# Loading the channel weights beside attention in three parts, in a fused attention, token-mixing and gating kernel

## The chip, the cores and the metric

One core of a Trainium2 chip runs the whole program. The metric is the device time in microseconds of one execution, as the median of several runs.

## What is computed

The input is attention over 2 batches of 12 heads (448 tokens, head size 64), then two mixing blocks. Cut to what matters here:

```python
x = attention(q, k, v)                                   # (2, 448, 768), causal
h = np.maximum(x.transpose(0, 2, 1) @ w_tok1, 0.0) @ w_tok2
u = x + h.transpose(0, 2, 1)
h2 = np.maximum(u @ w_ch1, 0.0) @ w_ch2                  # w_ch1: 768 x 1536
x = u + h2
# then a gated block with w_in, w_sg, w_out, and a residual
```

The first factor, `r = relu(u @ w_ch1)`, is what the change touches.

## The kernel before

Weights arrive as 64-bit words. `load_raw` (L104) issues one load of such words from SyncE's queue into a tile `wraw`, of which there are two. `decode` (L117) makes 32-bit numbers of them in a tile `wm` (three of them): an activation on ScalarE (L127), a shift on VectorE (L130) and a shift with an or on VectorE (L131). `load64` (L133) then makes a high part on ScalarE (L140) and, through `sub` (L100), a low part on GpSimd (L101). `load_w` (L143) does so for a slice of 128 columns of `w_ch1`: 128 partitions of 768 words, which is 768 KB of raw words, and gives `whi` and `wlo`.

`channel_up` and `up_third` multiply such a slice with `u`, which is kept as a high and a low part too, in `mm3` (L181): for each of six blocks `c` of 128 rows three matmuls, high by high (L185), high weight by low `u` (L186) and low weight by high `u` (L187), 18 in all into the PSUM tile `r_ps`.

Attention goes by pairs of heads. A head has two calls of `probabilities` (L324): scores on TensorE into `s_ps` (L345, two buffers), a mask with a running minimum on VectorE (L350), an exponential on ScalarE (L359), a half-precision high part on ScalarE (L371), its low part on GpSimd (L372, tile `hl`), and a transpose by DMA from SyncE's queue (L373) into `pT`. `values` (L383) multiplies `pT` with the values into `x_ps` (L396 to L398). At the end of a pair VectorE scales `x_ps` into `xf` (L424 to L426), and ScalarE and GpSimd split it into `xh` and `xl` (L429, L435, L101). After two pairs `token_mix` (L438) multiplies these into `a_ps` (L443, L444, and L185 to L187 from `mm3`), splits the result into `ah` and `al` (L448, L449) and multiplies again into `u_ps` (L459 to L468).

Eight of the twelve slices of `r` for batch 0 (`NF0`) are put beside the attention of batch 1. `up_third` (L495) is called from the fourth head of batch 1 on and multiplies two of the six blocks at a time. A scheduler orders the instructions of each engine by priorities and a timeline of its own. `tc.issue_after(ins)` adds an edge without a semaphore: what the block traces on the engine of `ins` stands behind `ins` on that engine. `marks` holds, for each head, the last DMA transpose issued by then; the load of slice `m` stands behind `marks[H - 2 + m]`. `tc.high_priority(offset=-LATER)` gives the load, the decode and the split of the slice a late priority.

Of the kernel before, what the change touches and what calls it, by code (L numbers as in the profile page):

```python
# [11 lines left out]
F32 = mybir.dt.float32  # L12
# [16 lines left out]
def mixer_kernel(  # L29
# [18 lines left out]
    nc = tc.nc  # L48
    B, H2, D2, S = q.shape
    H, D = 2 * H2, D2 // 2  # L50
# [3 lines left out]
    P = 128  # L54
# [5 lines left out]
    WC = 768  # L60
# [3 lines left out]
    LATER = 1500  # L64
# [5 lines left out]
    wpool = ctx.enter_context(tc.tile_pool(name="wpool", bufs=2))  # L70
# [29 lines left out]
    def sub(lo, src, hi):  # L100
        nc.gpsimd.tensor_sub(lo, src, f32(hi))  # L101
# [38 lines left out]
            nc.scalar.copy(hi, m)  # L140
        sub(lo, m, hi)

    def load_w(src, pool=wpool, bufs=3):  # L143

        k = src.shape[1]
        hi = pool.tile([P, WC // P, P], F32R, tag="whi", name="whi", bufs=bufs)[:, :k, :]
        lo = pool.tile([P, WC // P, P], F32R, tag="wlo", name="wlo", bufs=bufs)[:, :k, :]
        load64(hi.rearrange("p a f -> p (a f)"), lo.rearrange("p a f -> p (a f)"), src.rearrange("p a f -> p (a f)"))
        return hi, lo

    def absmax(dst, src):
# [65 lines left out]

    r_of = {}

    def channel_up(m, batches, pool, psum):  # L220

        wh, wl = load_w(w_ch1[m])
        for b in batches:
            us = slice(b * S, (b + 1) * S)
            pr = psum.tile([P, 512], F32, tag="d", name="r_ps")
            mm3(pr[:, :S], [((wh[:, c, :], wl[:, c, :]), (u_hi[c][b], u_lo[c][b])) for c in range(NCC)])
            r_done(m, b, pr, pool)
# [23 lines left out]
    with ExitStack() as at:  # L251
# [75 lines left out]
        def probabilities(qp, k2, hd, half, on_pe):  # L327

            ps = ps_s.tile([P, NP], F32, tag="s", name="s_ps")
            if (hd, half) == (1, 0):
                pe, mx = pes[count[0] % len(pes)], mxs[count[0] % len(pes)]
            else:
                pe = xp.tile([P, NP], F32, tag="pe", name="pe", bufs=NPE)
                mx = stp.tile([P, 2], F32, tag="mx", name="mx")
            todo, o = [], 0
            for j, i in enumerate(HALVES[half]):
                w = KW[i]
                if i > 0 or hd == 0:  # L340
                    todo.append((j, i, slice(o, o + w)))
                    q0 = S - 64 if i == 0 else S + w - P if hd else w - P - 64
                    for ks in KEYS[i]:
                        m = ks.stop - ks.start
                        last_s[0] = nc.tensor.matmul(ps[:, o:o + m], qp[:, q0:q0 + P], k2[:, ks], start=True, stop=True).ins  # L345
                        o += m
                else:
                    o += w
            for j, i, cs in todo:
                last_mx[0] = nc.vector.tensor_tensor_reduce(  # L350
                    out=pe[:, cs], in0=ps[:, cs], in1=mask0 if i == 0 else mask[:, MASKS[i]],
                    scale=-1.0 / math.sqrt(D), scalar=3.0e38, op0=ALU.add, op1=ALU.min, accum_out=mx[:, j:j + 1],
                ).ins
            bias = mx
            if not on_pe:
                bias = stp.tile([P, 2], F32, tag="bias", name="bias")
                nc.scalar.add(bias, mx, math.log(PSCALE))
            for j, i, cs in todo:
                nc.scalar.activation(pe[:, cs], pe[:, cs], AF.Exp, bias=bias[:, j:j + 1], scale=-1.0)  # L359
            pT = hlp.tile([P, 2, NP // P, P], F16, tag="pT", name="pT", bufs=4)  # L360
            if on_pe:
                tp = ps_e.tile([P, 512], F32, tag="d", name="t_ps")
                for c in range(NP // P):
                    cs = slice(c * P, (c + 1) * P)
                    nc.tensor.matmul(tp[:, cs], pe[:, cs], ident, is_transpose=True, start=True, stop=True)
                hi, lo = (pT[:, i].rearrange("p c q -> p (c q)") for i in range(2))
                nc.scalar.activation(hi, tp, AF.Copy, scale=PSCALE)
                nc.vector.scalar_tensor_tensor(lo, tp, PSCALE, hi, ALU.mult, ALU.subtract)
                return pT
            hl = hlp.tile([P, 2, NP], F16, tag="hl", name="hl", bufs=4)  # L370
            nc.scalar.copy(hl[:, 0], pe)  # L371
            nc.gpsimd.tensor_sub(hl[:, 1], pe, hl[:, 0])  # L372
            last[0] = nc.sync.dma_start_transpose(  # L373
                out=pT.rearrange("p a c q -> p (a c) q"), in_=hl.rearrange("p a n -> p (a n)")
            ).ins
            return pT


# [92 lines left out]
                nc.vector.tensor_sub(u_lo[cc][b], pu[:, :S], f32(u_hi[cc][b]))  # L471


        last, last_x, marks = [None], [None], []
        order = [(b, h) for b in range(B) for h in range(H)]
        qks, vss = {}, {}

# [14 lines left out]
        dense = list(range(NF0))  # L492
        thirds = []

        def up_third():  # L495

            if not thirds:
                m = dense.pop(0)
                with tc.issue_after(marks[H - 2 + m]), tc.high_priority(offset=-LATER):
                    wh, wl = load_w(w_ch1[m])  # L500
                pr = ps_e.tile([P, 512], F32, tag="d", name="r_ps")
                thirds.extend((m, pr, wh, wl, c) for c in range(0, NCC, 2))
            m, pr, wh, wl, c0 = thirds.pop(0)
            mm3(
                pr[:, :S],
                [((wh[:, c, :], wl[:, c, :]), (u_hi[c][0], u_lo[c][0])) for c in (c0, c0 + 1)],
                c0 > 0, not thirds,
            )
            if not thirds:
                r_done(m, 0, pr, rpool)  # L510

        def up():

            m = dense.pop(0)
            with tc.issue_after(marks[H - 2 + m]):
                channel_up(m, [0], rpool, ps_e)

        def decode_tok(c):
            with tc.issue_after(last_mx[0]), tc.high_priority(offset=-80):
# [11 lines left out]
        for n, (b, h) in enumerate(order):  # L531
            if n > 0:
                prepare(n + AHEAD)
                prepare_v(n + VAHEAD)
            if n == GH - 1:
                for c in range(2, NQ):
                    load_tok(c)
                for c in range(NT):
                    load_tok2(c)
            if h % GH == 0:  # L540
                x = (
                    xp.tile([P, GH // 2, 7, D], F32, tag="xf", name="xf", bufs=2),
                    xp.tile([P, NQ, GH * D], F32R, tag="xh", name="xh"),
                    xp.tile([P, NQ - 1, GH * D], F32R, tag="xl", name="xl"),
                )
            if h % 2 == 0:
                it = pair(b, h // 2, h % GH // 2, qks[b, h // 2], x, b == 0 and h > 0)
            next(it, None)
            marks.append(last[0])
            if h % GH == GH - 1:  # L550
                token_mix(b, h // GH, *x)

            if b == 1 and h >= 3:
                for _ in range(1 if h < H - 3 else 2):
                    up_third()
# [354 lines left out]
```

## Time and profile before

| | |
|---|---|
| runs before | 416.0, 416.13 and 414.38 us, median 416.0 |
| profiled execution | 416.44 us, its span 414.7 us |
| TensorE busy | 391.3 us (94%), mean granted clock 0.988 |
| GpSimd busy | 202.5 us (49%) |
| VectorE and ScalarE busy | 282.4 us (68%) and 250.4 us (60%) |

The profile is one execution. Its span leaves out 1.74 us of the time around it. The attention of both batches takes the first 169 us or so; after it come the other slices of `r`, the second channel product and the gated block. Shares over the whole span mix these stages, so they are read by stretches of time.

### The profile page before, as it was taken

Reading aid. Unit: us, or ns where it says so; the run is one execution under the profiler, and the core shown is the slowest. Engines: PE = TensorE matmul, PEld = TensorE weight load, DVE = VectorE, ACT = ScalarE, POOL = GpSimd, SP = SyncE. Lnnn points to the kernel's source line nnn. Section 1 sums busy time; section 2 is a strip of 40 time slices with the busy share of each in tenths; the row PEclk is TensorE's granted clock in tenths of the full one; section 3 lists DMA queues with packets and bytes.
Section 4 is the critical chain, followed back from the end, with each engine's and each line's share of the span. In section 5 each row is a group of like instructions: output and inputs, shape, how many; then the busy total and the mean of one; then the engine's idle time right before and its main releaser. Section 6 shows DMA issues by size and latency. Waiting matters only on the chain.

```text
span 414.7 us, 7332 instructions
## 1 busy us (share of the span) xinstructions
PE 391.3 (94%) x2622; PEld 267.9 (65%) x2622; DVE 282.4 (68%) x696; ACT 250.4 (60%) x483; POOL 202.5 (49%) x208
## 2 busy tenths in 40 slices
PE   5879899799898998999999999999999999999996
PEld 3447778588787887999889555555544445554554
DVE  6887866887785426444446787557898996469742
ACT  3988767787876555565679886344256556553210
POOL 3759864997686466062261447145121348315300
PEclk9999999799999999999999999999999999999999
DMA  7999899979997544466643313534623131100122
GB/s 220 246 238 232 161 206 271 246 186 236 265 247 140 137 112 144 163 217 229 207 149 102 90 65 114 186 107 134 222 73 90 51 103 51 52 2 0 68 92 107
DMA packets 61747, 61.77 MB, mean 149 GB/s; under 512 B 47888, under 2 KB 53264, under 8 KB 61712
## 3 DMA queue, kind: packets, MB, share of 16 engines
q1 hardware_dynamic: 61712, 61.32, 55.6%
q8 instruction: 20, 0.33, 0.3%
q14 instruction: 15, 0.12, 0.1%
HBM read 47.29 MB, written 2.75 MB: 121 GB/s over the span
## 4 chain that ended last, share of the span: by engine, by line
PE 25%; DVE 18%; ACT 12%; POOL 10%; DMA 9%; issue 8%; SPq 0%; POOLq 0%; ACTq 0%
DMA wraw<-in 7%; PE r_ps L186 5%; PE r_ps L185 5%; PE r_ps L187 5%; ACT r L172 3%; POOL hl L372 3%; PE o_ps L187 2%; PE o_ps L185 2%; PE o_ps L186 2%; DVE y L173 2%; DVE wm L131 2%; DVE w2m L131 1%; ACT wm L127 1%; PE u_ps L459 1%; POOL w L179 1%
## 5 line engine op out<-in xcount | busy, mean ns | idle before, releaser
L345 PE MATMUL s_ps<-k,q 128*128 128x64 f32 (+3 forms) x216 | 57.2, 405 | 11.5 <-DVE mx L350 4.8
L372 POOL TENSOR_TENSOR hl<-pe,hl 128x512 f16<-128x512 f32 x43 | 52.3, 1223 | 25.6 <-ACT hl L371 24.5
L101 POOL TENSOR_TENSOR wlo<-wm,whi 128x768 fp32r<-128x768 f32 x20 | 39.9, 1994 | 40.4 <-ACT whi L140 40.2
L185 PE MATMUL r_ps<-uh,whi 128*128 128x448 f32 x144 | 55.1, 383 | 0.0
L130 DVE TENSOR_SCALAR wm<-wm 128x768 int32<-128x768 int32 (+2 forms) x35 | 22.9, 655 | 46.9 <-ACT wm L127 46.9
L186 PE MATMUL r_ps<-ul,whi 128*128 128x448 f32 x144 | 53.9, 374 | 0.0
L187 PE MATMUL r_ps<-uh,wlo 128*128 128x448 f32 x144 | 53.0, 368 | 0.0
L185 PE MATMUL y_ps<-r,w 128*128 128x448 f16 x144 | 50.8, 353 | 0.0
L127 ACT ACTIVATE wm<-wraw 128x768 f32<-128x768 f32 (+2 forms) x35 | 27.8, 798 | 38.0 <-DMA wraw<-in 24.1
L186 PE MATMUL y_ps<-r,w 128*128 128x448 f16 x144 | 50.7, 352 | 0.0
L187 PE MATMUL y_ps<-r,w 128*128 128x448 f16 x144 | 50.6, 352 | 0.0
L345 PEld LDWEIGHTS s_ps<-k,q 128*128 128x128 f32 x216 | 32.2, 207 | 22.5 <-DVE mx L350 6.7
L350 DVE CUSTOM_DVE_ANT_0 pe<-s_ps,mask 128x192 f32<-128x192 f32 (+3 forms) x84 | 34.6, 441 | 7.2 <-PE s_ps L345 6.4
L246 POOL TENSOR_TENSOR y<-yt,ul 128x448 f32<-128x448 f32 x12 | 15.8, 1319 | 46.4 <-DVE yt L244 46.4
L359 ACT ACTIVATE pe<-pe,bias 128x448 f32<-128x448 f32 (+3 forms) x74 | 35.6, 525 | 0.4
L131 DVE SCALAR_TENSOR_TENSOR wm<-wraw,wm 128x768 int32<-128x768 int32 (+2 forms) x35 | 32.8, 938 | 0.7
L396 PE MATMUL x_ps<-vh,pT 128*128 128x65 f16 (+1 forms) x240 | 26.9, 201 | 3.1 <-DMA pT<-hl 3.0
L371 ACT CAST hl<-pe 128x512 f16<-128x512 f32 x43 | 26.3, 611 | 5.9 <-DMA pT<-hl 4.7
L185 PEld LDWEIGHTS r_ps<-uh,whi 128*128 128x128 f32 x144 | 27.3, 190 | 3.0 <-issue 0.4
L186 PEld LDWEIGHTS r_ps<-ul,whi 128*128 128x128 f32 x144 | 27.2, 189 | 3.1 <-issue 0.6
L187 PEld LDWEIGHTS r_ps<-uh,wlo 128*128 128x128 f32 x144 | 27.2, 189 | 2.7 <-issue 0.2
L179 POOL TENSOR_TENSOR w<-w2m,w 128x768 f16<-128x768 f32 x12 | 21.2, 1787 | 15.8 <-ACT w L178 11.2
(212 smaller groups left out, 1016.0 us busy)
## 6 DMA issues: line engine op xcount, KB each, us to landing
wraw<-in SPq DMA_DIRECT2D x36, 768.0 KB, 4.5
wraw<-in SPq DMA_DIRECT2D x14, 512.0 KB, 3.8
vr<-in SPq DMA_DIRECT2D x12, 320.0 KB, 4.0
k<-in SPq DMA_DIRECT2D x12, 224.0 KB, 3.7
q<-in SPq DMA_DIRECT2D x24, 112.0 KB, 4.0
out<-ob SPq DMA_DIRECT2D x11, 224.0 KB, 1.9
wraw<-in SPq DMA_DIRECT2D x3, 256.0 KB, 4.6
pT<-hl SPq DMA_TRANSPOSE x43, 4.0
```

What stands on the lines that cost most here:

```text
L101: nc.gpsimd.tensor_sub(lo, src, f32(hi))
L127: nc.scalar.activation(m, words.bitcast(F32)[:, :, 1], AF.Prelu, scale=2.0 ** -112, alpha=-(2.0 ** 32))
L131: nc.vector.scalar_tensor_tensor(mi, words[:, :, 0], 29, mi, ALU.logical_shift_right, ALU.bitwise_or)
L185: nc.tensor.matmul(ps, lh, rh, start=i == 0 and not begun, stop=False)
L186: nc.tensor.matmul(ps, lh, rl, start=False, stop=False)
L187: done.append(nc.tensor.matmul(ps, ll, rh, start=False, stop=ended and i == n - 1).ins)
L345: last_s[0] = nc.tensor.matmul(ps[:, o:o + m], qp[:, q0:q0 + P], k2[:, ks], start=True, stop=True).ins
L350: last_mx[0] = nc.vector.tensor_tensor_reduce(out=pe[:, cs], in0=ps[:, cs], in1=mask0 if i == 0 else mask[:, MASKS[i]], scale=-1.0 / math. ...
L359: nc.scalar.activation(pe[:, cs], pe[:, cs], AF.Exp, bias=bias[:, j:j + 1], scale=-1.0)
L371: nc.scalar.copy(hl[:, 0], pe)
L372: nc.gpsimd.tensor_sub(hl[:, 1], pe, hl[:, 0])
L396: nc.tensor.matmul(o, ph, vh[:, c, h, :D + 1], start=j == 0, stop=False)
```

## The change

`load_parts` is new. With `behind` given, `load_w` loads a slice in three parts of 256 words per partition, each behind a DMA transpose of its own, and these three transposes follow each other. The raw tile is the same, and so are `decode` and the high part: one operation each over 768 columns. The low part is made by three operations of 256 columns. `marks` now holds the place in the list `turns` of all transposes, and `turns_from(n)` gives three of them from there on. This holds for the eight slices beside attention; all other weights are loaded as before.

```diff
+    def load_parts(src, behind):
+        raw = wpool.tile([P, WC], mybir.dt.int64, tag="wraw", name="wraw", bufs=2)
+        w = WC // len(behind)
+        for i, ins in enumerate(behind):
+            cs = slice(i * w, (i + 1) * w)
+            with tc.issue_after(ins):
+                nc.sync.dma_start(raw[:, cs], src[:, cs])
+        return raw
...
-    def load_w(src, pool=wpool, bufs=3):
+    def load_w(src, pool=wpool, bufs=3, behind=None):
...
-        load64(hi.rearrange("p a f -> p (a f)"), lo.rearrange("p a f -> p (a f)"), src.rearrange("p a f -> p (a f)"))
+        src, hi1, lo1 = (t.rearrange("p a f -> p (a f)") for t in (src, hi, lo))
+        if behind is None:
+            load64(hi1, lo1, src)
+        else:
+            m = wpool.tile([P, WC], F32, tag="wm", name="wm", bufs=3)
+            decode(m, src, raw=load_parts(src, behind))
+            nc.scalar.copy(hi1, m)
+            w = WC // len(behind)
+            for i in range(len(behind)):
+                cs = slice(i * w, (i + 1) * w)
+                sub(lo1[:, cs], m[:, cs], hi1[:, cs])
...
-            last[0] = nc.sync.dma_start_transpose(
+            turns.append(nc.sync.dma_start_transpose(
...
+        def turns_from(n):
+            return [turns[min(marks[n] + i, len(turns) - 1)] for i in range(3)]
+
         def up_third():
...
-                with tc.issue_after(marks[H - 2 + m]), tc.high_priority(offset=-LATER):
-                    wh, wl = load_w(w_ch1[m])
+                with tc.high_priority(offset=-LATER):
+                    wh, wl = load_w(w_ch1[m], behind=turns_from(H - 2 + m))
...
-            with tc.issue_after(marks[H - 2 + m]):
-                channel_up(m, [0], rpool, ps_e)
+            channel_up(m, [0], rpool, ps_e, turns_from(H - 2 + m))
...
-            marks.append(last[0])
+            marks.append(len(turns) - 1)
```

Since the scheduler sets the order, the diff shows little of what moves. Three places follow. The numbers behind the names tell buffers apart; lines past L143 are those of each kernel's own file (L373 before is L393 now, L113 for these loads is L150).

**Place 1**, SyncE's queue and then VectorE, where the first slices are loaded, at about 63 to 79 us of the profile. `wraw_1667` holds slice 0, `wraw_1932` (now `wraw_1936`) slice 1, `wraw_2228` slice 2. The queue before:

```order
L113 DMA wraw_1667<-in_5 128x768
L113 DMA wraw_1932<-in_5 128x768
L306 DMA vr_1467<-in_2 128x640
L298 DMA k2_1463<-in_1 128x448
L373 DMA_TRANSPOSE pT_1343<-hl_1344 128x8x128
L373 DMA_TRANSPOSE pT_1378<-hl_1379 128x8x128
L300 DMA q0_163<-in_0 64x448
L113 DMA wraw_2228<-in_5 128x768
L373 DMA_TRANSPOSE pT_1404<-hl_1405 128x8x128
L373 DMA_TRANSPOSE pT_1433<-hl_1434 128x8x128
```

and now:

```order
L150 DMA wraw_1667<-in_5 128x256 x2
L150 DMA wraw_1936<-in_5 128x256
L326 DMA vr_1467<-in_2 128x640
L318 DMA k2_1463<-in_1 128x448
L393 DMA_TRANSPOSE pT_1343<-hl_1344 128x8x128
L393 DMA_TRANSPOSE pT_1378<-hl_1379 128x8x128
L320 DMA q0_163<-in_0 64x448
L150 DMA wraw_1667<-in_5 128x256
L150 DMA wraw_1936<-in_5 128x256
L393 DMA_TRANSPOSE pT_1404<-hl_1405 128x8x128
L393 DMA_TRANSPOSE pT_1433<-hl_1434 128x8x128
```

Three parts stand ahead of the first two transposes instead of two whole loads, and two parts ahead of the next two instead of a whole load. VectorE before (`wm_1666` and `wm_1931` are the decodes of slices 0 and 1, `s_ps_1480` and `s_ps_1514` are scores):

```order
L130 TENSOR_SCALAR wm_1666<-wm_1666 128x768
L131 SCALAR_TENSOR_TENSOR wm_1666<-wraw_1667,wm_1666 128x768
L471 TENSOR_TENSOR ul2_0_110<-u_ps_932,uh2_0_98 128x448
L313 TENSOR_REDUCE am_1469<-vr_1467 128x1
L130 TENSOR_SCALAR wm_1931<-wm_1931 128x768
L424 TENSOR_SCALAR rd_1249<-x_ps_1126,sv_968 128x7
L318 TENSOR_REDUCE sv_1322<-vm_1320 128x1
L131 SCALAR_TENSOR_TENSOR wm_1931<-wraw_1932,wm_1931 128x768
L350 ISA pe_1481,mx_1482<-s_ps_1480,mask0_86 128x64
```

and now:

```order
L446 TENSOR_TENSOR xf_974<-x_ps_1126,rd_1249 128x448
L370 ISA pe_1481,mx_1482<-s_ps_1480,mask0_86 128x64
L370 ISA mx_1482 128x1
L340 RECIPROCAL sv_1322<-sv_1322 128x1
L370 ISA pe_1481,mx_1482<-s_ps_1480,mask_87 128x448
L370 ISA mx_1482 128x1
L130 TENSOR_SCALAR wm_1666<-wm_1666 128x768
L370 ISA pe_1515,mx_1516<-s_ps_1514,mask_87 128x192
```

The decodes of slices 0 and 1 stood ahead of the masks of `s_ps_1480`; now slice 0 stands behind these masks, ahead of those of `s_ps_1514`, and slice 1 comes later still.

**Place 2**, GpSimd, where the low parts of slices 2 and 3 meet the attention of the third pair of batch 1 (its `x_ps` is number 1700 before, 1704 now), at about 85 to 104 us of the profile. Before, with `wlo_2226` for slice 2:

```order
L101 TENSOR_TENSOR wlo_2226<-wm_2227,whi_2225 128x768
L372 TENSOR_TENSOR hl_1527<-pe_1515,hl_1527 128x512
L372 TENSOR_TENSOR hl_1553<-pe1_156,hl_1553 128x512
L372 TENSOR_TENSOR hl_1582<-pe_1570,hl_1582 128x512
L372 TENSOR_TENSOR hl_1713<-pe_1702,hl_1713 128x512
L372 TENSOR_TENSOR hl_1748<-pe_1736,hl_1748 128x512
L372 TENSOR_TENSOR hl_1780<-pe0_155,hl_1780 128x512
L372 TENSOR_TENSOR hl_1809<-pe_1797,hl_1809 128x512
```

and now, with `wlo_2234` for slice 2 and `wlo_2336` for slice 3:

```order
L101 TENSOR_TENSOR wlo_2234<-wm_2235,whi_2233 128x256 x3
L101 TENSOR_TENSOR xh_1329<-xf_1328,xh_1329 64x64
L392 TENSOR_TENSOR hl_1717<-pe_1706,hl_1717 128x512
L101 TENSOR_TENSOR xl_1330<-xf_1328,xh_1329 128x3x128
L392 TENSOR_TENSOR hl_1752<-pe_1740,hl_1752 128x512
L101 TENSOR_TENSOR wlo_2336<-wm_2337,whi_2335 128x256 x3
L392 TENSOR_TENSOR hl_1784<-pe0_155,hl_1784 128x512
L455 TENSOR_SCALAR xh_1329<-xf_1328 64x64 x2
L392 TENSOR_TENSOR hl_1813<-pe_1801,hl_1813 128x512
```

The four low parts of the third pair stood in a row; now the low parts of two slices, and splits of `xf`, stand among them. The three operations of a slice follow each other here, as they do for all eight slices.

**Place 3**, GpSimd and then TensorE at the last token mix (`xh_2083`, now `xh_2091`), at about 156 to 166 us of the profile. GpSimd before (`wlo_2566` is slice 7; the next two are slices 0 and 1 for batch 1):

```order
L372 TENSOR_TENSOR hl_2376<-pe_2364,hl_2376 128x512
L101 TENSOR_TENSOR wlo_2566<-wm_2567,whi_2565 128x768
L101 TENSOR_TENSOR wlo_2661<-wm_2662,whi_2660 128x768
L435 TENSOR_SCALAR xh_2083<-xf_2082 64x64 x2
L101 TENSOR_TENSOR xh_2083<-xf_2082,xh_2083 64x64
L101 TENSOR_TENSOR wlo_2692<-wm_2693,whi_2691 128x768
```

and now (`wlo_2559` is slice 6, `wlo_2594` slice 7):

```order
L101 TENSOR_TENSOR wlo_2559<-wm_2560,whi_2558 128x256 x3
L455 TENSOR_SCALAR xh_2091<-xf_2090 64x64 x2
L101 TENSOR_TENSOR xh_2091<-xf_2090,xh_2091 64x64 x2
L101 TENSOR_TENSOR xl_2092<-xf_2090,xh_2091 128x3x128
L101 TENSOR_TENSOR wlo_2594<-wm_2595,whi_2593 128x256 x3
L101 TENSOR_TENSOR wlo_2693<-wm_2694,whi_2692 128x768
```

No low part stands among the last splits any more. TensorE before (`r_ps_2575` is slice 7):

```order
L187 MATMUL r_ps_2575<-uh5_0_104,wlo_2566 128x448
L443 MATMUL a_ps_2405<-xh_2083,w1h_151 128x256
L444 MATMUL a_ps_2405<-xh_2083,w1l_152 128x256
L185 MATMUL a_ps_2405<-xh_2083,w1h_151 128x256
L186 MATMUL a_ps_2405<-xl_2084,w1h_151 128x256
```

and now (`r_ps_2537` is slice 5, `r_ps_2572` slice 6):

```order
L207 MATMUL r_ps_2537<-uh5_0_104,wlo_2524 128x448
L463 MATMUL a_ps_2421<-xh_2091,w1h_151 128x256
L464 MATMUL a_ps_2421<-xh_2091,w1l_152 128x256
L205 MATMUL a_ps_2421<-xh_2091,w1h_151 128x256
L205 MATMUL r_ps_2572<-uh0_0_94,whi_2558 128x448
L206 MATMUL r_ps_2572<-ul0_0_106,whi_2558 128x448
L207 MATMUL r_ps_2572<-uh0_0_94,wlo_2559 128x448
L205 MATMUL r_ps_2572<-uh1_0_96,whi_2558 128x448
```

All eight slices were done before the last token mix; now slices 6 and 7 are still to be multiplied there: six matmuls of slice 6 stand between the third matmul into `a_ps` and the first that reads `xl`, and 23 matmuls of slices 6 and 7 between the last into `a_ps` and the first into `u_ps`.

## Rows read from the trace of the kernel before

**Rows 1.** Busy time by stretches: bounds, length, engines (instructions), TensorE's clock, DMA share, GB/s.

```profile
72.00:84.00 12.00, 9.65 (x81) 7.05 (x81) 10.24 (x33) 9.37 (x21) 11.31 (x14) 0.72 1.09 249
84.00:98.00 14.00, 14.00 (x121) 11.78 (x120) 10.52 (x26) 10.93 (x26) 11.52 (x10) 1.00 0.86 190
98.00:110.00 12.00, 10.31 (x125) 8.63 (x123) 9.66 (x26) 9.63 (x22) 8.35 (x13) 1.00 1.08 224
...
160.00:169.00 9.00, 7.17 (x46) 6.17 (x45) 4.68 (x4) 3.28 (x6) 3.99 (x4) 1.00 0.48 164
169.00:350.00 181.00, 180.52 (x924) 114.78 (x923) 127.43 (x270) 111.25 (x186) 72.36 (x52) 1.00 0.41 130
```

**Rows 2.** TensorE's waits from 72 to 170 us: us in total, times, longest.

```profile
PE x_ps L396 <- DMA pT<-hl: 3.0, 2, 1.7
PE s_ps L345 <- DVE mx L350: 2.3, 2, 2.0
PE u_ps L459 <- ACT ah L448: 0.7, 1, 0.7
PE a_ps L443 <- POOL xh L101: 0.7, 1, 0.7
PE a_ps L186 <- POOL xl L101: 0.5, 1, 0.5
```

**Rows 3.** VectorE's timeline where those scores wait: start us, us, what.

```profile
74.00 0.94 DVE L131 SCALAR_TENSOR_TENSOR wm<-wraw,wm 128x768 int32<-128x768 int32 x1
```

**Rows 4.** SyncE's timeline: start us, us for issuing, what, how many.

```profile
63.77 1.05 SPq L113 DMA_DIRECT2D wraw<-in  x2
67.08 5.50 SPq L373 DMA_TRANSPOSE pT<-hl  x2
81.77 1.24 SPq L373 DMA_TRANSPOSE pT<-hl  x1
99.22 1.06 SPq L113 DMA_DIRECT2D wraw<-in  x2
100.40 6.57 SPq L373 DMA_TRANSPOSE pT<-hl  x2
```

**Rows 5.** SyncE's own waits from 60 to 150 us: us in total, times, longest.

```profile
SPq L373 <- POOL hl L372: 22.8, 11, 6.0
SPq L113 <- DVE wm L131: 2.4, 3, 1.6
```

**Rows 6.** Line 101 of GpSimd, and line 113 from 60 to 150 us: ns min/median/max.

```profile
L101 POOL TENSOR_TENSOR wlo<-wm,whi x20: 1819/1859/2502, 75.2 to 219.8; 128x768 fp32r<-128x768 f32 x20
L101 POOL TENSOR_TENSOR w1l<-wm,w1h x4: 727/754/1312, 9.4 to 24.5; 128x256 fp32r<-128x256 f32 x4
...
L113 SPq DMA_DIRECT2D wraw<-in x12: 328/446/683, 63.8 to 149.9; - x12
```

**Rows 7.** The page's DMA issues: count, KB each, median us from issue to landing.

```profile
wraw<-in SPq DMA_DIRECT2D x36, 768.0 KB, 4.5
...
wraw<-in SPq DMA_DIRECT2D x3, 256.0 KB, 4.6
```

**Rows 8.** TensorE's timeline, two waits and two plain matmuls: start us, us, what, idle before.

```profile
109.51 0.20 PE L396 MATMUL x_ps<-vh,pT 128*128 128x65 f16 x1 [1.69 <-DMA pT<-hl]
...
133.39 0.20 PE L396 MATMUL x_ps<-vh,pT 128*128 128x65 f16 x1 [1.31 <-DMA pT<-hl]
...
158.94 0.37 PE L187 MATMUL r_ps<-uh,wlo 128*128 128x448 f32 x1
159.15 0.37 PE L185 MATMUL r_ps<-uh,whi 128*128 128x448 f32 x1
```

**Rows 9.** GpSimd's timeline ahead of the second wait and at the last token mix.

```profile
127.86 1.17 POOL L372 TENSOR_TENSOR hl<-pe,hl 128x512 f16<-128x512 f32 x1 [0.54 <-ACT hl L371]
...
158.93 1.84 POOL L101 TENSOR_TENSOR wlo<-wm,whi 128x768 fp32r<-128x768 f32 x1
...
161.25 1.01 POOL L101 TENSOR_TENSOR xl<-xf,xh 128x384 fp32r<-128x384 f32 x1
```

More of the change, by code (lines that the diff above doesn't have):

```diff
@@ L218, in mixer_kernel, with channel_up @@
     r_of = {}
-    def channel_up(m, batches, pool, psum):
-        wh, wl = load_w(w_ch1[m])
+    def channel_up(m, batches, pool, psum, behind=None):
+        wh, wl = load_w(w_ch1[m], behind=behind)
         for b in batches:
@@ L372, in probabilities @@
             nc.gpsimd.tensor_sub(hl[:, 1], pe, hl[:, 0])
-            last[0] = nc.sync.dma_start_transpose(
+            turns.append(nc.sync.dma_start_transpose(
                 out=pT.rearrange("p a c q -> p (a c) q"), in_=hl.rearrange("p a n -> p (a n)")
-            ).ins
+            ).ins)
             return pT
@@ L471, in token_mix @@
                 nc.vector.tensor_sub(u_lo[cc][b], pu[:, :S], f32(u_hi[cc][b]))
-        last, last_x, marks = [None], [None], []
+        turns, last_x, marks = [], [None], []
         order = [(b, h) for b in range(B) for h in range(H)]
@@ L498, in up_third @@
                 m = dense.pop(0)
-                with tc.issue_after(marks[H - 2 + m]), tc.high_priority(offset=-LATER):
-                    wh, wl = load_w(w_ch1[m])
+                with tc.high_priority(offset=-LATER):
+                    wh, wl = load_w(w_ch1[m], behind=turns_from(H - 2 + m))
                 pr = ps_e.tile([P, 512], F32, tag="d", name="r_ps")
```

## Prediction

> **What bounds the kernel now.** I read the busy time by stretches first [rows 1]. From 169 to 350 us TensorE is busy for 180.52 of 181 us: whatever comes there sooner moves the end with it, as long as the work is the same, and the change leaves the matmuls as they are. So the question is when TensorE has done all matmuls of attention and the eight slices of `r` beside it, at 169 us now. Between 72 and 169 us it loses time in a few places only, and the table of waits names them [rows 2]: 3.0 us for transposes, 2.3 us for the masks on VectorE, 1.9 us (0.7, 0.7 and 0.5) at the token mixes. A second loss does not show as a wait: in 72 to 84 us the granted clock is 0.72 in the mean [rows 1], of which (1 - 0.72) x 12 = 3.4 us is what a clock at 1.2 instead of 2.4 GHz may have cost there. The engine had stood idle for 2.0 us in a row for the masks just before. Ahead of 72 us the two programs are the same.
>
> Next come the engines that feed attention. GpSimd is busy for 11.31 of 12 us in 72 to 84 us, 11.52 of 14 and then 8.35 of 12 [rows 1]. DMA has a share of 1.09, 0.86 and 1.08. In SyncE's timeline [rows 4] two whole loads at 63.77 us are followed by two transposes that take 5.50 us to issue, and two more loads at 99.22 us by two that take 6.57 us; one that stands clear takes 1.24 us. A load ahead thus holds the queue for transposes: (5.50 - 2.48) / 2 = 1.5 to (6.57 - 2.48) / 2 = 2.0 us for each load. Mostly, though, the transposes wait for `hl` on GpSimd, 22.8 us in 11 waits [rows 5].
>
> **The change part by part.** All sums go against the profiled execution, 416.44 us (span 414.7, 1.74 around it). It stands 0.44 us above the median of the runs shown, so I take 0.44 off at the end.
>
> Issues: eight loads become 24. That is 16 more issues of 0.446 us (0.328 to 0.683) [rows 6], 7.1 us of SyncE's queue over some 80 us. The bytes are the same. Cover: SyncE mostly waits for `hl`; without it the 7.1 us would come ahead of transposes.
>
> Low parts: three operations of 754 ns instead of one of 1859 ns [rows 6], so 2262 - 1859 = 0.40 us more for a slice and 3.2 us for eight, all on GpSimd. It has 2.5 + 3.7 = 6.1 us of idle time in 84 to 110 us [rows 1], next to none before. The scheduler keeps the three together, so no `hl` slips in between; all that a part gains is that the matmuls of the first two blocks may start 1.5 us (two operations) ahead of the last.
>
> Early stall (place 1). The 2.3 us for masks come from two decodes in front of them, the later one 0.94 us long at 74.00 us [rows 3]. They now stand behind the masks of those scores. Instead, the next masks stand behind the first shift of slice 0 on VectorE, whose third part leaves SyncE two transposes later: a new wait, with those masks and thereby a later `hl` behind it. Ahead of these two transposes stand 768 KB instead of 1536, so they should leave about one load's hold, 1.5 us, sooner. Bounds: 5.7 us won (wait and clock) to nothing won, since the new wait can be as long as the old. I take the row that names the stall, **2.3 us won**, and leave the clock where it is, since transposes may now be what TensorE waits for.
>
> Middle (place 2). Ahead of the last `hl` of the third pair stand the low part of slice 3 (2.26 us) and an `xl` (1.01 us [rows 9]) that came after it, and the extra 0.40 us of slices 0 to 2: 2.26 + 1.01 + 1.2 = 4.5 us later on GpSimd. The wait at 109.51 us, 1.69 us now [rows 8], is for the transpose of this very `hl`. Bounds: nothing (the transpose no longer stands behind two whole loads, which held it for 4.1 us) to 4.5 us lost. GpSimd's idle 2.5 us in 84 to 98 us takes its part: **2.0 us lost**.
>
> Later wait, at 133.39 us, 1.31 us [rows 8]. Its `hl` starts at 127.86 us [rows 9]. In the new order it stands ahead of two `xl` of 1.01 us that came before it. Bounds 0 and 1.31; **1.0 us won**.
>
> Last token mix (place 3). TensorE's 1.9 us there [rows 2] come while GpSimd makes a low part of 1.84 us at 158.93 us, with `xl` behind it at 161.25 us [rows 9]. Now no low part stands there, six matmuls of slice 6 fill the wait for `xl` and 23 the wait for `ah`; at 0.21 us each (158.94 to 159.15 us [rows 8]) that is 1.2 and 4.8 us of cover for 0.5 and 0.7. Only the first wait, for `xh`, has none but an earlier `xh`. Bounds 0 and 1.9; **1.6 us won**. If slice 7's low part comes late, its matmuls wait instead; it stands right behind `xl`, 2.3 us of work.
>
> Sum: -2.3 + 2.0 - 1.0 - 1.6 = -2.9, so 413.5 us in the terms of the profiled execution, and **413.1 us** as a median.
>
> **The rivals.** *Given back* (415.6 us): the whole 4.5 us of the middle reach TensorE, 2.5 more than taken, which leaves -0.4. For it: the `hl` of that pair stand behind two slices; against it: GpSimd is idle for 2.5 us there. It decides if the last `hl` of the third pair is not on GpSimd before 102 us.
>
> *Held queue*, slower (419.3 us): the first part of a slice waits for a raw tile that the decode two slices back has not freed, at the head of SyncE's queue, with transposes behind it. Before, that wait was 2.4 us in three, the longest 1.6 [rows 5]. If each of slices 2 to 7 waits 1.6 us, 9.6 us come ahead of transposes. The transposes behind the loads at 99.22 us were 4.1 us late, and TensorE waited 1.69 for them, 0.41 of it; 0.41 x 9.6 = 3.9 us. The early 2.3 us are then not won either: -2.9 + 2.3 + 3.9 = +3.3. For it: the decodes now come later on VectorE. Against it: two raw tiles were enough before. It decides once a decode ends after the next but one slice's first part has reached the head.
>
> *Too many small loads*, slower (418.3 us): the 7.1 us of issues stand on the path as those transposes did, 0.41 x 7.1 = 2.9, and the early 2.3 are not won: +2.3. Rows speak for it in one point: 256 KB took 4.6 us to land and 768 KB 4.5 [rows 7], so a third is not done in a third of the time; against it, parts in flight overlap. The Trainium skill (DMA: Bandwidth & Descriptors, Rules for kernel authors) asks for at least 1 MiB per DMA and to coalesce many small transfers, which speaks against this change. The two landing times agree with it; by the rule this rival would be the forecast. I give it little, since the loads are not what TensorE waits for [rows 2].
>
> *Clock kept too* (409.7 us): the early stall goes without a new one, and the clock's 3.4 us with it: -2.9 - 3.4 = -6.3.
>
> **How the numbers follow.** Forecast 0.42, given back 0.23, held queue 0.16, small loads 0.06, clock kept 0.13. About 0.5%, 2.1 us, is what a measurement of this kernel can tell from no change, so the edge of faster is 413.9 us. The forecast's own spread, 411.5 to 415 us, puts 0.32 of its 0.42 beyond that edge. Faster: 0.32 + 0.13 = 0.45. Same: 0.10 + 0.23 = 0.33. Slower: 0.16 + 0.06 = 0.22. The range goes from 409.0, below the clock case, to 418.6, which takes in the small loads and leaves out most of the held queue. Cases of both signs hold much of the chance; the likeliest alone has 411.5 to 415.
>
> **What would show it.** Right: no wait of `s_ps` for masks at 73 to 76 us; the wait for `hl`'s transpose near 109 us still there, 2 to 5 us; no wait of `a_ps` or `u_ps` at the last token mix beyond 0.5 us; the stretch without idle time begins at about 166 us. Held queue: line 150 on SyncE waits for VectorE's line 131 for 5 us or more in total. Clock kept: a granted clock of 1.00 from 72 to 84 us. Wrong altogether if TensorE waits for `wlo` (line 207) beside attention, or if the time after 169 us changes by itself.

## The result and the profile after

The change made the kernel slower. In nine runs the median was 417.23 us (416.36 to 418.42), against 415.06 us (414.23 to 416.13) of nine runs of the kernel before: a ratio of 1.0055 [1.0039, 1.0072]. It was run twice more beside the experiments: 1.0021 [0.9994, 1.0047] and 1.0057 [1.0034, 1.0079]. The mean of the three, 1.0044, is 1.8 us. These ratios, and those below, leave out executions over 1.5% longer than the fastest of their kernel (one each of e4, e8 and e13). The forecast was 413.1 us: the time lies in the wide range, and the sign is wrong.

The profiled execution took 417.71 us, its span 415.8 us. Its busy time by stretches, with the columns of [rows 1]:

```profile
72.00:84.00 12.00, 8.87 (x95) 6.95 (x94) 8.29 (x22) 7.64 (x16) 6.89 (x10) 0.86 0.94 230
84.00:98.00 14.00, 12.26 (x115) 10.21 (x115) 10.15 (x27) 10.00 (x21) 11.17 (x14) 1.00 1.00 238
98.00:110.00 12.00, 7.80 (x72) 5.12 (x71) 9.98 (x35) 10.27 (x24) 8.87 (x12) 1.00 0.97 212
110.00:142.00 32.00, 32.00 (x284) 28.00 (x284) 20.98 (x53) 22.78 (x51) 21.98 (x27) 0.95 0.78 188
142.00:160.00 18.00, 18.00 (x152) 16.35 (x151) 5.71 (x9) 10.50 (x20) 13.47 (x19) 1.00 0.35 103
160.00:169.00 9.00, 9.00 (x50) 8.32 (x49) 4.41 (x7) 3.63 (x8) 1.84 (x1) 1.00 0.59 194
169.00:350.00 181.00, 180.02 (x919) 114.26 (x918) 128.68 (x268) 111.91 (x189) 74.84 (x52) 1.00 0.41 134
```

The last row's stretch is the one that was taken to move as a whole. From 110 to 169 us TensorE now has no idle time, where it had waited at 133 us and at the last token mix. From 84 to 110 us it lost 14.00 - 12.26 + 12.00 - 7.80 = 5.94 us, against 1.69 before. Its waits from 72 to 170 us, the answer to [rows 2]:

```profile
PE x_ps L416 <- DMA pT<-hl: 7.9, 5, 2.6
PE s_ps L365 <- DVE sv L339: 0.8, 1, 0.8
PE x_ps L416 <- DVE mx L370: 0.2, 1, 0.2
PE x_ps L416 <- DVE xf L446: 0.2, 1, 0.2
```

The wait for masks has gone and transposes have taken its place. TensorE's timeline has the longer ones (start us, us, what, idle before):

```profile
77.11 0.23 PE L416 MATMUL x_ps<-vh,pT 128*128 128x65 f16 x1 [2.60 <-DMA pT<-hl]
...
96.57 0.20 PE L416 MATMUL x_ps<-vh,pT 128*128 128x65 f16 x1 [1.74 <-DMA pT<-hl]
...
109.49 0.20 PE L416 MATMUL x_ps<-vh,pT 128*128 128x65 f16 x1 [2.56 <-DMA pT<-hl]
```

For the first of them, SyncE's timeline and GpSimd's:

```profile
65.91 4.38 SPq L393 DMA_TRANSPOSE pT<-hl  x2
70.34 0.58 SPq L320 DMA_DIRECT2D q<-in  x1
70.98 2.17 SPq L150 DMA_DIRECT2D wraw<-in  x2
73.26 2.59 SPq L393 DMA_TRANSPOSE pT<-hl  x2
```

```profile
68.25 1.16 POOL L392 TENSOR_TENSOR hl<-pe,hl 128x512 f16<-128x512 f32 x1 [0.86 <-ACT hl L391]
```

These `hl` were ready by 69.41 us and are transposed from 73.26 us on, behind two transposes that take 4.38 us to issue, a load of `q` and two parts. For the last of the three waits, GpSimd's timeline over the third pair and one row of ScalarE's:

```profile
95.11 1.15 POOL L392 TENSOR_TENSOR hl<-pe,hl 128x512 f16<-128x512 f32 x1
...
99.85 1.16 POOL L392 TENSOR_TENSOR hl<-pe,hl 128x512 f16<-128x512 f32 x1 [2.63 <-ACT hl L391]
101.90 2.31 POOL L101 TENSOR_TENSOR wlo<-wm,whi 128x256 fp32r<-128x256 f32 x3 [0.90 <-ACT whi L164]
104.18 1.16 POOL L392 TENSOR_TENSOR hl<-pe,hl 128x512 f16<-128x512 f32 x1
...
105.95 1.16 POOL L392 TENSOR_TENSOR hl<-pe,hl 128x512 f16<-128x512 f32 x1
```

```profile
98.34 0.93 ACT L127 ACTIVATE wm<-wraw 128x768 f32<-128x768 f32 x1 [2.71 <-DMA wraw<-in]
```

GpSimd waits 2.63 us for an `hl` of ScalarE, which stands there behind a decode operation that waited 2.71 us for a part, and then a low part of 2.31 us goes ahead of the next `hl`.

Behind attention there is a wait that the profile of the kernel before does not have:

```profile
217.35 0.22 PE L185 MATMUL rs_ps<-ident_b,ram 128*128 128x128 bf16 x1
...
277.24 0.36 PE L207 MATMUL y_ps<-r,w 128*128 128x448 f16 x1 [0.18 <-POOL w L199]
```

This first `rs_ps` is taken as a mark of how far TensorE is: in every kernel here the same 1022 matmuls start from it on. In the kernel before it is at 217.13 us:

```profile
217.13 0.22 PE L165 MATMUL rs_ps<-ident_b,ram 128*128 128x128 bf16 x1
```

From there to the end of the span it is 415.8 - 217.35 = 198.45 us; before, 414.7 - 217.13 = 197.57.

### The profile page after: what moved, and what is told of

The parts are those of the page before. It is cut to its first block, busy times and chain, and to the rows that moved or that the text cites. A ratio compares the mean times of both kernels' runs of the same rounds, so it can differ in the third digit from the quotient of the medians.

```text
span 415.8 us, 7374 instructions
## 1 busy us (share of the span) xinstructions
PE 389.4 (94%) x2622; PEld 266.7 (64%) x2622; DVE 281.5 (68%) x696; ACT 250.9 (60%) x483; POOL 205.1 (49%) x224
## 4 chain that ended last, share of the span: by engine, by line
PE 22%; DVE 17%; DMA 12%; ACT 12%; POOL 8%; issue 7%; SPq 0%; POOLq 0%; ACTq 0%
DMA wraw<-in 11%; ACT r L192 3%; DVE w2m L131 3%; PE o_ps L207 2%; PE o_ps L205 2%; PE o_ps L206 2%; PE r_ps L205 2%; PE r_ps L206 2%; PE r_ps L207 2%; DVE y L193 2%; PE u_ps L479 2%; POOL wlo L101 2%; DVE wm L131 2%; DVE w2m L130 2%; POOL w L199 2%
## 5 line engine op out<-in xcount | busy, mean ns | idle before, releaser
L365 PE MATMUL s_ps<-k,q 128*128 128x64 f32 (+3 forms) x216 | 54.7, 393 | 10.9 <-DVE mx L370 4.6
L101 POOL TENSOR_TENSOR wlo<-wm,whi 128x256 fp32r<-128x256 f32 (+1 forms) x36 | 44.1, 1246 | 39.2 <-ACT whi L140 35.0
L365 PEld LDWEIGHTS s_ps<-k,q 128*128 128x128 f32 x216 | 31.0, 199 | 21.7 <-DVE mx L370 5.6
L131 DVE SCALAR_TENSOR_TENSOR wm<-wraw,wm 128x768 int32<-128x768 int32 (+2 forms) x35 | 31.9, 913 | 0.7
L416 PEld LDWEIGHTS <-pT 128*128 128x128 f16 (+1 forms) x240 | 21.3, 98 | 16.0 <-DMA pT<-hl 10.6
```

Of the source, the lines that this page charges most:

```text
L131: nc.vector.scalar_tensor_tensor(mi, words[:, :, 0], 29, mi, ALU.logical_shift_right, ALU.bitwise_or)
L416: nc.tensor.matmul(o, ph, vh[:, c, h, :D + 1], start=j == 0, stop=False)
```

## The experiments

All ratios are to the kernel before, run on the same chip. The theories as first put: **A**, ScalarE stands at a slice's first decode operation until the third part has landed, with `hl` queued behind it. **B**, the low part in three operations delays `hl` on GpSimd. **C**, 24 issues stand in front of transposes on SyncE.

### One part of the change at a time

e1, the low part in one operation:

```diff
-            w = WC // len(behind)
-            for i in range(len(behind)):
-                cs = slice(i * w, (i + 1) * w)
-                sub(lo1[:, cs], m[:, cs], hi1[:, cs])
+            sub(lo1, m, hi1)
```

> The three-part load of the change, but the low part made in one operation as before; ScalarE's order is that of the changed kernel up to the first r. Theory A (ScalarE stands at the first decode operation of a slice, line 127, until the part behind the third transpose has landed, with hl, exponentials and xh queued behind it; 9.7 us of such waits in 62 to 170 us): 416.5 to 418.0 us, still about 2 us above before, and ScalarE still waits 8 us or more for wraw. Rival B (the three low-part operations delay hl on GpSimd): 415.0 to 415.6 us, the loss gone. Rival C (24 issues on SyncE's queue): 416.5 to 418.0 us.

Measured: 1.0029 [1.0004, 1.0055]. ScalarE waited 8.6 us for `wraw` from 62 to 170 us. Some loss stays, and the interval takes in the change's, so neither A nor B falls.

e2, one whole load, the low part in three:

```diff
-        w = WC // len(behind)
-        for i, ins in enumerate(behind):
-            cs = slice(i * w, (i + 1) * w)
-            with tc.issue_after(ins):
-                nc.sync.dma_start(raw[:, cs], src[:, cs])
+        with tc.issue_after(behind[0]):
+            nc.sync.dma_start(raw, src)
```

> One whole load behind one transpose as before, but the low part in three operations. Theory A: 414.5 to 415.9 us, within 0.8 us of before; ScalarE waits about 4 to 7 us for wraw in 62 to 170 us, as before. Rival B: 416.3 to 417.5 us. Rival C: 414.5 to 415.6 us.

Measured: 1.0016 [0.9992, 1.0040]. Three operations alone are not the loss, though they may be up to 0.4%.

e3, all three parts behind one transpose, and e4, all parts two transposes earlier:

```diff
-            return [turns[min(marks[n] + i, len(turns) - 1)] for i in range(3)]
+            return [turns[marks[n]]] * 3                     # e3
+            return [turns[marks[n] + i - 2] for i in range(3)]  # e4
```

> Three parts, but all three behind the transpose that released the whole load before; three low-part operations, 24 issues. Theory A: 413.5 to 415.9 us, ScalarE's waits for wraw at 6 us or less, since the last part no longer waits for two more transposes. Rival B: 416.3 to 417.5 us. Rival C: 416.5 to 418 us.

> Three parts behind three successive transposes, as in the change, but all two transposes earlier, so that the third part leaves where the whole load left before; three low-part operations, 24 issues. Theory A: 413.0 to 415.9 us, ScalarE's waits for wraw at 6 us or less. Rival B: 416.3 to 417.5 us. Rival C: 416.5 to 418 us.

Measured: e3 1.0057 [1.0028, 1.0086], with ScalarE's waits for `wraw` down to 5.0 us in the same stretch; e4 0.9989 [0.9962, 1.0016], with 7.4 us of them. A would have e3 no slower than before. C falls with e4, which issues the same 24 parts and makes the same three low parts, and is not slower; so does B as the count of operations. What e4 changes is where in the order the slices stand.

### The place on GpSimd

Theory **D**: what counts is how much of the slices' work stands among the 25th to 30th `hl` on GpSimd, of the second and third pair. GpSimd's time for `wlo` between the start of the 24th and of the 31st `hl`, of the kernel before, then of the change (bounds, length, engines as in [rows 1], of instructions with `wlo` alone; GpSimd is the third with a count):

```profile
80.60:96.69 16.09, 1.59 (x4) 0.89 (x4) 1.83 (x1) 0.90 0.84 213
```

```profile
78.46:105.95 27.49, 2.20 (x6) 1.13 (x6) 8.99 (x12) 0.97 0.96 236
```

These seven `hl` take 27.49 us instead of 16.09, with 8.99 us of low parts between them instead of 1.83. e5 moves the low parts of three slices on GpSimd alone, ScalarE's order staying; e6 moves decodes on ScalarE too (`casts` and `subs` are lists of ScalarE's and GpSimd's `hl` instructions):

```diff
+        PRE, LOW = {}, {1: 27, 2: 27, 3: 30}                          # e5
+        PRE, LOW = {0: 23, 3: 28, 4: 30}, {1: 27, 2: 27, 3: 30}       # e6
+        def late(m):
+            return casts[PRE[m]] if m in PRE else None, subs[LOW[m]] if m in LOW else None
...
+            with tc.issue_after(late[0]) if late[0] else nullcontext():
+                decode(m, src, raw=raw)
...
+                with tc.issue_after(late[1]) if late[1] else nullcontext():
+                    sub(lo1[:, cs], m[:, cs], hi1[:, cs])
```

> The changed kernel with the low parts of slices 1, 2 and 3 queued later on GpSimd alone, behind the 28th, 28th and 31st hl instead of the 26th, 27th and 29th; ScalarE's order is untouched. Theory D (what counts is how many low parts and conversions of slices stand among the 25th to 30th hl, the second and third pair of the second batch, on GpSimd above all: four in the changed kernel, one in the kernel before): 1.000 to 1.003 of before, TensorE's waits for transposes in 84 to 112 us down from 5.0 us to about 3. Rival A (ScalarE's wait for the third part): 1.004 to 1.007, waits unchanged. Rival C (parts on SyncE's queue in front of transposes): 1.004 to 1.007.

> As the run before, and in addition the first decode operation of slices 0, 3 and 4 on ScalarE behind the 24th, 29th and 31st hl conversion instead of the 23rd, 28th and 28th. Theory D: 0.998 to 1.003. Rival A: 0.997 to 1.002 and ScalarE's wait for wraw under 4 us in 72 to 110 us, from 9.7. Rival C: 1.004 to 1.007.

Measured: e5 0.9999 [0.9971, 1.0026], TensorE's waits for transposes in 84 to 112 us 2.7 us instead of 5.0, as D expected, though with its other waits TensorE still loses 4.2 us there instead of 5.9. e6 1.0030 [1.0004, 1.0056], although ScalarE waits only 2.6 us for `wraw` from 72 to 112 us instead of 9.7. That speaks against A, though the interval still reaches A's 1.002; D had 1.003 at most.

e7 joins e4 and e1 (two transposes earlier, one low-part operation); e18 is the same again. e8 is `turns[marks[n] + i - 3]`; e11 that with one low-part operation; e12 is e11 with slice 2's low part behind the 29th `hl`.

> Three parts two transposes earlier than in the change, with the low part in one operation; the low parts stand behind the 23rd, 23rd, 26th and 32nd hl, nearly as before (23rd, 23rd, 24th and 32nd). Theory D: 0.995 to 1.001. Rival A: 0.995 to 1.001. Rival C: 1.004 to 1.007, since the 24 issues remain.

> Three parts behind three successive transposes, three transposes earlier than in the change; low parts in three operations behind the 22nd, 23rd, 25th and 32nd hl. Theory D: 0.996 to 1.002. Rival A: 0.996 to 1.002, since the data comes earlier still. Rival C: 1.004 to 1.007. If the raw tile is not free at the head of SyncE's queue by then: 1.003 to 1.010, with line 150 waiting 3 us or more.

> Three parts three transposes earlier than in the change, and the low part in one operation, behind the 22nd, 23rd, 25th and 31st hl. Theory D: 0.992 to 0.998, no worse than the same with three operations. Rival C: 1.004 or more.

> As the run before, with slice 2's low part queued behind the 29th hl on GpSimd instead of the 25th. Theory D: 0.990 to 0.997, up to 1 us better than the run before, as one low part less stands among the hl of the second and third pair. If the place on GpSimd no longer matters here: within 0.2% of the run before.

> All parts two transposes earlier and the low part in one operation, as once before: 0.994 to 0.999 of before if it beats both kernels; 0.999 to 1.002 if the first result was chance.

Measured: e7 0.9965 [0.9938, 0.9993], e18 0.9981 [0.9958, 1.0003], e8 0.9975 [0.9946, 1.0003], e11 1.0001 [0.9976, 1.0026], e12 0.9975 [0.9949, 1.0002]. e11 missed what D expected, and e12 by 0.0005. ScalarE's waits from 72 to 112 us in e7:

```profile
ACT wm L127 <- DMA wraw<-in: 8.5, 4, 3.7
```

Nearly the change's 9.7 us, in the fastest version of all. With e3, e6 and e7 A has fallen: ScalarE may wait this long for these parts and the kernel loses nothing. GpSimd's row for `wlo` in e7, to be held against the two above:

```profile
81.80:100.00 18.20, 1.46 (x4) 0.69 (x4) 1.91 (x1) 1.00 1.11 246
```

e9 is the change again, e10 the mirror: the kernel before, with nothing but the low parts of slices 0 to 2 queued where the change has them.

```diff
+        LOW = {0: 23, 1: 25, 2: 26}
...
+        with tc.issue_after(late) if late else nullcontext():
+            sub(lo, m, hi)
```

> The changed kernel as it is, beside the three others on one chip, so that its ratio can be set beside theirs: 1.003 to 1.007 by every theory.

> The kernel before, with whole loads and one low-part operation; only the low parts of slices 0, 1 and 2 are queued later on GpSimd, behind the 24th, 26th and 27th hl, where the change has them, instead of the 23rd, 23rd and 24th. Theory D: 1.003 to 1.007, the loss without a single part-load. Rivals A and C (the loss comes from the late third part or from the 24 issues): 0.998 to 1.002. If the early place of the low parts was itself a cost (GpSimd full in 72 to 84 us): 0.994 to 0.998.

Measured: e9 1.0021 [0.9994, 1.0047], below the 1.003 to 1.007 that every theory gave; e10 1.0007 [0.9984, 1.0029]. D missed here: 6.79 us of low parts among those `hl` cost 0.3% at most when the loads and decodes stay as they were. The place of these three on GpSimd alone is not enough for the whole loss. The low part of slice 3, which the change has behind the 29th `hl`, stayed behind the 32nd in e10.

### The eighth slice

e9's profile has a longer wait for `w`:

```profile
215.87 0.22 PE L185 MATMUL rs_ps<-ident_b,ram 128*128 128x128 bf16 x1
...
276.63 0.36 PE L207 MATMUL y_ps<-r,w 128*128 128x448 f16 x1 [1.06 <-POOL w L199]
```

TensorE came to `rs_ps` 1.26 us sooner than in the profile before, and the span still ended 0.6 us later. Theory **E**: in the change the eighth slice of `r` is multiplied among and behind the last token mix, so its buffers come free late and with them everything decoded behind it, up to `w`. e13 writes the last slices ahead of that token mix; e14 is the change on the same chip, e15 one execution of the kernel before.

```diff
+            if n == len(order) - 1:
+                while dense:
+                    up()
             if h % GH == GH - 1:
                 token_mix(b, h // GH, *x)
...
-                    up_third()
+                    if dense or thirds:
+                        up_third()
```

> The changed kernel, with the last three slices of r beside attention written ahead of the last token mix: the eighth slice's 18 matmuls then stand ahead of its u_ps, as in the kernel before, instead of 11 ahead, 4 among and 3 behind. ScalarE, GpSimd, VectorE and SyncE keep their order up to the last token mix. Theory E: 0.5 to 1.5 us faster than the change on this chip, no wait of y_ps for w near 276 us (0.18 and 1.06 us in the change's two profiles), and 197.0 to 197.8 us from the rs_ps matmul to the end of the span instead of 198.4 to 199.4. Theory D (all of the loss lies in 84 to 112 us of attention): within 0.4 us of the change, 198 us or more from rs_ps to the end.

> The changed kernel as it is, for the comparison on this chip: 1.002 to 1.006 of before. Theory E expects a wait of y_ps for w again, 0.1 to 1.1 us; theory D only the waits for transposes in 84 to 112 us, 3.5 to 5.5 us.

> The kernel before as it is, one look: both theories expect 1.7 us (0.5 to 2.5) of waits for transposes in 84 to 112 us. Theory E expects no wait of y_ps for w beyond 0.2 us and 197 to 198 us from rs_ps to the end.

Measured: e13 1.0067 [1.0034, 1.0100], e14 1.0057 [1.0034, 1.0079]. e13 has no wait for `w`, and 197.9 us from `rs_ps` to the end, but it uncovers another:

```profile
168.47 0.55 PE L479 MATMUL u_ps<-w2h,ah 128*128 128x448 f32 x1 [2.40 <-ACT ah L468]
```

So e13 brings no gain: the 23 matmuls of slices 6 and 7 behind `a_ps` had been the cover for `ah`. Nor does it show E's mechanism, since TensorE came to `rs_ps` 3.0 us later than in e14 (221.60 against 218.59 us) and would have found `w` anyway if that had stayed where it was. e14 waits 0.7 us for `w` and takes 199.0 us from `rs_ps` to the end; e15 does not wait for `w` and takes 197.55.

e16 and e17 ask whose lateness counts. Two transposes earlier go the parts of slices 0 to 3 in e16, of slices 4 to 7 in e17:

```diff
+            back = 2 if n < H + 2 else 0     # e16; e17: n >= H + 2
+            return [turns[min(marks[n] + i - back, len(turns) - 1)] for i in range(3)]
```

> The change, with the parts of slices 0 to 3 two transposes earlier and those of 4 to 7 where the change has them; the eighth slice's 18 matmuls stand between a_ps and u_ps, none behind. Theory E: 0.997 to 1.002 of before, 197.0 to 197.9 us from rs_ps to the end, no wait of y_ps for w over 0.3 us. If it is the last four slices' loads that count: 1.003 to 1.007, as the change.

> The change, with the parts of slices 4 to 7 two transposes earlier and those of 0 to 3 where the change has them; TensorE's order is that of the change to the last matmuls, with 3 of the eighth slice behind the last u_ps. Theory E: 1.003 to 1.007, 198.3 to 199.5 us from rs_ps to the end, and a wait of y_ps for w. If it is the last four slices' loads that count: 0.997 to 1.002.

Measured: e16 1.0003 [0.9981, 1.0025], e17 1.0068 [1.0041, 1.0096]. **The loss belongs to the parts of the first four slices**: e16 differs from the change in these alone, e17 in those of the last four alone, and e17 keeps the loss. For E e16 is a miss nevertheless. The eighth slice stands ahead of `u_ps` in it, and TensorE waits for `w` all the same, and longer:

```profile
213.46 0.22 PE L185 MATMUL rs_ps<-ident_b,ram 128*128 128x128 bf16 x1
...
275.14 0.36 PE L207 MATMUL y_ps<-r,w 128*128 128x448 f16 x1 [1.41 <-POOL w L199]
```

It reaches `rs_ps` 3.67 us before the kernel before and `w` is not there. From `rs_ps` to the end it takes 200.9 us, where E had 197.9 at most, so nearly all of the lead is given back, 1.41 us of it at `w`. e10 waits for `w` as well, although all its eight slices are multiplied ahead of the last token mix, as in the kernel before:

```profile
276.57 0.36 PE L188 MATMUL y_ps<-r,w 128*128 128x448 f16 x1 [0.52 <-POOL w L180]
```

With that E has fallen as a cause: the eighth slice's place is not needed for the wait. It comes when TensorE is early against `w`, and the kernel before is close to it. There GpSimd ends this `w` at 276.34 us, 0.33 us before the matmul that reads it:

```profile
274.50 1.84 POOL L179 TENSOR_TENSOR w<-w2m,w 128x768 f16<-128x768 f32 x1 [4.55 <-issue]
276.67 0.35 PE L187 MATMUL y_ps<-r,w 128*128 128x448 f16 x1
```

GpSimd's rows for `wlo` among the same `hl`, of e16, then of e17:

```profile
81.40:95.70 14.30, 0.74 (x2) 0.38 (x2) 3.40 (x3) 1.00 0.91 222
```

```profile
78.70:104.80 26.10, 2.19 (x6) 1.13 (x6) 10.14 (x12) 0.93 1.01 244
```

e17's profile happened to be the shortest of its runs (415.4 us, median 418.49), so its waits are not read as typical.

All kernels in the order of that row's GpSimd time:

| GpSimd, us | kernels and ratios |
|---|---|
| 1.8 to 2.2 | before 1, e12 0.9975, e7 0.9965, e18 0.9981, e2 1.0016 |
| 2.5 to 3.4 | e11 1.0001, e8 0.9975, e4 0.9989, e16 1.0003 |
| 4.6 | e3 1.0057 |
| 6.6 to 7.9 | e5 0.9999, e10 1.0007, e1 1.0029, e6 1.0030 |
| 9.0 to 10.1 | the change 1.0055, 1.0021, 1.0057, e13 1.0067, e17 1.0068 |

The order is one of single profiles, and neighbouring rows overlap within their intervals. Only e3 is clearly out of line; why is open (its profile has a wait of 2.1 us for `ul` and one of 2.9 us for a transpose at 121.67 us).

## Why the prediction was wrong

The sum, term by term, against the profiles of the change (three) and of the kernel before (two), in us:

| term | forecast | measured |
|---|---|---|
| early stall, 72 to 84 us | -2.3 | 3.1, 2.4, 3.1 against 2.3, 2.4: +0.5 |
| middle, 84 to 112 us | +2.0 | 6.0, 5.8, 5.2 against 1.7, 1.9: +3.9 |
| waits from 112 to 170 us | -1.0 - 1.6 | none against 3.2, 5.0: -4.1 |
| from `rs_ps` to the end | 0 | 198.45, 199.43, 199.01 against 197.57, 197.55: +1.4 |
| around the span | 0 | 2.0 against 1.8: +0.2 |
| sum | -2.9 | +1.9 |

**Early stall: the failed step is "I take the row that names the stall, 2.3 us won".** The masks no longer wait, as foreseen, and nothing was won: the other bound, "nothing won, since the new wait can be as long as the old", was the answer. I looked for the new wait on VectorE. It came from TensorE's own order, which the prediction had not looked at there. Two of the four transposes of this pair did leave SyncE sooner, as forecast: the second has been issued by 75.85 us, and by 78.70 us before. But the pair's matmuls into `x_ps`, which read them, stood behind eight matmuls of scores, and now three quarters of them stand ahead of these. The kernel before (SyncE, then TensorE):

```profile
73.94 4.76 SPq L373 DMA_TRANSPOSE pT<-hl  x2
75.75 1.02 PE L345 MATMUL s_ps<-k,q 128*128 128x448 f32 x2 [2.00 <-DVE mx L350]
77.13 2.26 PE L345 MATMUL s_ps<-k,q 128*128 128x128 f32 x6 [0.35 <-DVE mx L350]
79.31 0.27 PE L396 MATMUL x_ps<-vh,pT 128*64 128x65 f16 x2
```

and TensorE now:

```profile
72.82 0.23 PE L416 MATMUL x_ps<-vh,pT 128*64 128x65 f16 x2 [0.23 <-DVE mx L370]
77.75 1.84 PE L365 MATMUL s_ps<-k,q 128*128 128x448 f32 x2
```

TensorE begins with these matmuls 6.5 us sooner and finds the third transpose still on the way. Two parts and a load of `q` stand in front of it on SyncE: I had counted the queue's 7.1 us of issues and set them beside SyncE's waits for `hl`, but a wait covers an issue only where it stands in front of it. ScalarE's line 127 waited 4.20 us at 74.64 us too; the `hl` of TensorE's wait at 77.11 us were done before that, so this is not what it waited for.

**Middle: mis-sized, 3.9 instead of 2.0,** near the upper bound of 4.5. The last `hl` of the third pair is on GpSimd at 105.95 us, past the 102 us from which *given back* was to decide, and 9.3 us later than before, where the sum had 4.5. The step that failed is "GpSimd's idle 2.5 us in 84 to 98 us takes its part". That idle time was there for ScalarE's `hl`, as GpSimd's rows of the kernel before show, and the delay of that `hl` came on top:

```profile
92.59 1.17 POOL L372 TENSOR_TENSOR hl<-pe,hl 128x512 f16<-128x512 f32 x1 [0.71 <-ACT hl L371]
94.95 1.16 POOL L372 TENSOR_TENSOR hl<-pe,hl 128x512 f16<-128x512 f32 x1 [1.19 <-ACT hl L371]
96.69 1.16 POOL L372 TENSOR_TENSOR hl<-pe,hl 128x512 f16<-128x512 f32 x1 [0.58 <-ACT hl L371]
```

Of the slices I had seen one (slice 3) move in among the third pair's `hl`; slice 2's low part stands ahead of the first of these, and not among them as place 2 says. In the order of the change the low parts of slices 0 to 3 stand among those of the second and third pair, and e16 and e17 show that the lateness of the first four slices' loads carries the loss.

**Waits after 112 us: right in sign,** 4.1 us won where 2.6 were forecast. Six matmuls and 23 matmuls did cover `xl` and `ah`; without them the wait for `ah` is 2.40 us in e13 and 0.7 in the kernel before. No run separates this cover from the 4 us by which TensorE came later, which by itself leaves its inputs more time.

**After 169 us: the failed step is "whatever comes there sooner moves the end with it".** TensorE was busy there, but a second path, the decode of the weights up to `w`, ran 0.33 us behind it. The text had named this ("if the time after 169 us changes by itself") and given it no chance. The waits for `w` are 0.2, 1.1 and 0.7 us in the three profiles of the change; in e16 such a wait takes back 1.41 us of what TensorE had gained. Another 0.35 us stands behind the last matmul: from its end to the end of the span it is 3.49 to 3.50 us in the change and 3.14 to 3.15 before. So it is in all profiles: 3.4 to 3.6 us in the 12 with three low-part operations, 3.1 to 3.2 in the eight with one. Why is open.

**The rivals.** *Given back*: its middle was nearly right, 3.9 of 4.5 us lost. Its time, 415.6, is too low, since it took the early 2.3 us as won and the end as it was. *Held queue*: line 150 waited 0.6 us for VectorE's line 131, not 5; its named mechanism was absent, though its time, 419.3, is on the right side. Line 113, the whole loads behind the eight slices, did wait 8.6 us for it, but after 112 us, where TensorE waits for nothing. *Small loads*: refuted by e4, e8 and e16, which keep the 24 parts and are not slower. A part lands in less time than a whole load, not the same:

```profile
wraw<-in SPq DMA_DIRECT2D x28, 768.0 KB, 4.2
```

```profile
wraw<-in SPq DMA_DIRECT2D x27, 256.0 KB, 3.5
```

So the rule that was cited (the Trainium skill, DMA: Bandwidth & Descriptors, Rules for kernel authors) had the sign and not the reason: no loss here goes with the size of the transfers. *Clock kept*: the clock was 0.86 in 72 to 84 us, better than 0.72, and 0.95 in 110 to 142 us, where it had been 1.00. Its sign, 1.00 from 72 to 84 us, came in e9, whose span is 415.3 us all the same; and e15, the kernel before, has 1.00 there too, with a span of 413.8 us instead of 414.7. So the 3.4 us went with the execution and not with the kernel. Over the change's first nine runs its mean was 0.993, over the 35 runs of the kernel before beside e1 0.993 as well. That is no difference to carry the loss.

**What stays open**: how much of the loss goes through GpSimd's low parts (e5, the table), how much through the decodes and loads that move with them (e10 says that the low parts alone are not all), and how much through TensorE's order, which moves with them too. Nor was it tried what sets the time of `w`. The chain of work that ended last in the change's profile leaves TensorE at 168.58 us and reaches `w` at 275.34 us through six loads of whole slices, 3.78 to 4.28 us each, with decodes between them.

Parts that leave two transposes earlier, with the low part in one operation (e7, e18), beat the change and, by about 1 us, the kernel before: 0.9965 [0.9938, 0.9993] and 0.9981 [0.9958, 1.0003], of which the second alone does not exclude 1.

## What to carry to other kernels

When a load is spread behind later events, everything made from it moves later too; look on each engine for what it then stands in front of, slice by slice, before pricing the load itself. A wait that a row names is only won if what TensorE does next is ready by then too, so read TensorE's order after the change and look when the input of each next matmul lands. And a stretch in which one engine is always busy may have a second path just behind it: look how late its last input came before counting every gain through to the end.

## What was not expected

- ScalarE's waits for the parts, 8.5 us from 72 to 112 us, stand in the fastest kernel, e7; the change has 9.7 us of them and e6, slower than before, 2.6.
- Two paths end side by side: TensorE's `y` and GpSimd's `w`. With TensorE 3.67 us ahead at `rs_ps` (e16) the wait for `w` was 1.41 us; in both profiles of the kernel before there is none, by 0.33 us.
- The time around the span is 1.86 to 2.15 us in the change's first nine runs and 1.73 to 1.86 us in 35 runs of the kernel before beside e1. e1 and e13 have about 2.0 too, e16 to e18 1.8. What sets it was not tried.
